# Attention, soft mixture of experts and MLP in one kernel: an eleventh load slot during attention, the last scores written where P will stand, two buffers for transposed P, and another order

## The chip, the cores and the metric

The program runs on one core of a Trainium2 chip. A core has a matrix engine (PE, with its weight loads shown as PEld), a vector engine (DVE), a scalar engine (ACT), a general engine (POOL) and a sequencer (SP) that here issues every DMA transfer. Each engine works through its own list of instructions in order and waits on semaphores. The metric is the device time of one execution in microseconds (us); lower is better.

## The reference, cut to what matters

```python
def _attn_ref(q, k, v):                 # q, k, v: 8 batches, 8 heads, 576 rows, 64 columns
    k_p = k.reshape(B, H, Sp, pool, D).mean(axis=3)      # 576 rows pooled to 72
    v_p = v.reshape(B, H, Sp, pool, D).mean(axis=3)
    scores = scale * np.matmul(q, k_p.transpose(0, 1, 3, 2))
    scores = scores - np.max(scores, axis=-1, keepdims=True)
    attn = np.exp(scores)
    attn = attn / (np.sum(attn, axis=-1, keepdims=True) + 1e-09)
    return np.matmul(attn, v_p)
def _moe_ref(x, phi, w1, w2):           # x: 4608 tokens of 512; 8 experts of 4 slots, F = 1024
    logits = x @ phi
    d = softmax of logits over the tokens; slot_input = d.T @ x
    for e in range(E):
        slot_out[e] = np.maximum(slot_input[e] @ w1[e], 0.0) @ w2[e]
    c = softmax of logits over the slots; return c @ slot_out
def _moe2_ref(x, w_in, w_out, s, b):    # 512 to 2048 to 512
    g = s * np.maximum(x @ w_in, 0.0) ** 2 + b
    return g @ w_out
```

## The kernel before, in words

Three stages follow each other on the same core: attention up to about 161 us, the experts (MoE) up to about 200 us, and the MLP to the end.

**Attention** goes over 36 tiles of 128 rows, t = 0 to 35, nine for each pair of batches (`pr, u = divmod(t, 9)`). A tile passes six steps, each a function. `st_A`: PE transposes q, ACT copies it to `qT`. `st_B`: PE multiplies with the pooled k (`kb`), DVE takes the maximum of each row (L413) and writes scores less maximum to `S` (L415). `st_C`: ACT takes the exponential in place (L423), DVE sums each row (L424) and inverts the sum (L426), POOL multiplies the two into P (L444). `S` has two buffers, for even and odd t, each with a 73rd column of 1e-9 behind the 72 scores, so that one sum over 73 columns gives the sum of the reference. P stands in six pair tiles `P2_0` to `P2_5` (two tiles of rows each) or in `Pm` (u = 0). `st_D`: PE transposes P, ACT copies it to `PT`. `st_E`: every second tile or so, PE multiplies two transposed tiles with `vpf` (pooled v already multiplied with phi), and ACT copies to `LT`. `st_F`: PE transposes that, DVE sums it into the logits `L`. `PT` has three buffers (`t % 3`), so that `st_D` of the next tile may stand ahead of the `st_E` that still reads the two before it.

After a batch's last F, `dispatch(b)` (a generator that is stepped by the letter r, or 6 and 7 for the last two batches) forms the slot inputs of that batch: PE L583, L588, L616 and L640 with DVE and ACT between. `prep(pr)` (stepped by p) pools k and v of the next pair: three additions for each chunk (L278, L282, L283), each chunk on POOL or DVE by a string such as PLAN1 (`kg0`: k chunk 0 on POOL; `kd1`: k chunk 1 on DVE; `K0`, `V0`: PE transposes of that chunk, L293).

The order of all this is written out by hand: FIRST and LOOP give the letters for each tile up to t = 27, TAIL for the rest. W3 in TAIL is three filler matmuls (L267) of the identity, which compute nothing.

**Loads.** All loads stand in one list, `loads`, and `pump()` issues its head as soon as a slot of 8 KB per partition is free; nothing passes the head. There are ten slots `ring` and three slots `raw` from the start. When the last reader of a pool of attention's tiles is written, TAIL closes the pool (Z: `pp1`, Y: `apb`, X1: `sc2`, X4: `apd`, X2: `apc`, X3: `apq`) and opens XR slots `x` over it, 3, 2, 1, 1 and 1 in the order Z, Y, X1, X4, X2; X3 opens a slot `brief`, and a second one follows behind attention. That makes 23 slots for the first 23 of the experts' 32 loads of 1 MB each. The other nine, and the first blocks of w_in and w_out, go into slots that the experts' matmuls set free.

**Experts.** The 32 weight blocks are taken in the order EORD: `w1` blocks with L1033, `w2` blocks with L1046 (into `sp_ps`) up to block NDIR - 1, and with L1049 (into `so_ps`, already folded) from NDIR on; L1021 adds what `sp_ps` held to `so_ps`. BEHIND says what else stands behind a block: t0 to t5 are PE transposes for the MLP (L968), c0 to c3 what these need, i and o conversions of w_in and w_out, and w2 two filler matmuls (L1015).

**MLP.** From L918 and L1136 on, PE goes through 96 steps of 18 matmuls (L1196) to the end.

## Time and profile before

| | |
|---|---|
| median of 3 runs | 643.15 us (642.7 to 644.52) |
| profiled execution, its own time | 644.16 us |
| span of that execution (first to last instruction) | 642.4 us |
| mean granted PE clock | 0.994 of full speed |
| busy: PE, DVE, ACT, POOL | 621.9, 450.1, 405.6, 303.4 us |
| bytes moved | 89.00 MB |

The profile shows one execution. A row of its timeline gives the start and the duration in us, the engine, the line of the kernel, the operation, the tiles that it writes and reads, how many such instructions are merged, and in brackets how long the engine had stood idle before and what ended that. Full PE clock is 2.4 GHz; 0.50 is 1.2 GHz. A matmul in f32 is shown as two rows, so eight rows are four matmuls.

### The profile page before, as it was taken

Reading aid. Unit: us, or ns where it says so; the run is one execution under the profiler, and the core shown is the slowest. Engines: PE = TensorE matmul, PEld = TensorE weight load, DVE = VectorE, ACT = ScalarE, POOL = GpSimd, SP = SyncE. Lnnn points to the kernel's source line nnn. Section 1 sums busy time; section 2 is a strip of 40 time slices with the busy share of each in tenths; the row PEclk is TensorE's granted clock in tenths of the full one; section 3 lists DMA queues with packets and bytes.
Section 4 is the critical chain, followed back from the end, with each engine's and each line's share of the span. In section 5 each row is a group of like instructions: output and inputs, shape, how many; then the busy total and the mean of one; then the engine's idle time right before and its main releaser. Section 6 shows DMA issues by size and latency. Waiting matters only on the chain.

```text
span 642.4 us, 13303 instructions
## 1 busy us (share of the span) xinstructions
PE 621.9 (97%) x5355; PEld 503.1 (78%) x5355; DVE 450.1 (70%) x722; ACT 405.6 (63%) x668; POOL 303.4 (47%) x241
## 2 busy tenths in 40 slices
PE   8879999998998999999999999999999999999997
PEld 7767778887545888888888888888888888888886
DVE  5768787897693787877658788967657554657444
ACT  3468788874374887756666656665656666565552
POOL 2987899534145344513153345351315332999100
PEclk9979999999999999999999999999999999999999
DMA  9999977679996202101111104021000000223323
GB/s 329 400 326 368 362 256 267 240 287 350 379 408 242 66 2 67 66 0 66 65 27 42 64 1 132 0 67 66 1 0 1 1 1 2 98 99 99 98 98 99
DMA packets 37389, 89.00 MB, mean 139 GB/s; under 512 B 6992, under 2 KB 15440, under 8 KB 37328
## 3 DMA queue, kind: packets, MB, share of 16 engines
q1 hardware_dynamic: 37328, 88.16, 38.4%
q8 instruction: 42, 0.69, 0.4%
q14 instruction: 19, 0.16, 0.1%
HBM read 78.71 MB, written 9.44 MB: 137 GB/s over the span
## 4 chain that ended last, share of the span: by engine, by line
PE 83%; DMA 6%; SPq 3%; DVE 3%; ACT 3%; issue 1%; POOL 1%; DVEq 0%; ACTq 0%; POOLq 0%
PE o L1196 61%; PE h L1136 5%; DMA x<-in_moe_w_dram 3%; PE l L1033 2%; PE sc L409 2%; SPq L152 2%; PE w L463 2%; DMA ring<-in_k_dram 2%; PE w L385 1%; PE w L616 1%; DMA qm<-in_q_dram 1%; PE w L489 1%; SPq L245 1%; POOL P L444 1%; PE w L514 1%
## 5 line engine op out<-in xcount | busy, mean ns | idle before, releaser
L1196 PE MATMUL o<-whi,gh 128*128 128x512 f32 x574 | 224.3, 391 | 0.6 <-DVE gh L1122 0.6
L1196 PE MATMUL o<-wlo,gh 128*128 128x512 f32 x574 | 224.0, 390 | 0.0
L1196 PE MATMUL o<-whi,gl 128*128 128x512 f32 x574 | 208.9, 391 | 0.0
L1164 DVE TENSOR_TENSOR gl<-r,gh 128x768 fp32r<-128x768 f32 (+1 forms) x97 | 105.8, 1092 | 112.1 <-ACT gh L1156 110.9
L1148 ACT ACTIVATE r<-h 128x768 f32<-128x768 f32 x94 | 76.7, 816 | 141.1 <-PE h L1136 139.2
L875 POOL TENSOR_TENSOR fr<-fr,xp 128x512 f32<-128x512 f32 x28 | 45.3, 1618 | 176.8 <-ACT fr L874 156.4
L1196 PEld LDWEIGHTS o<-whi,gl 128*128 128x128 f32 x574 | 107.7, 188 | 23.1 <-DVE gl L1164 0.4
L1196 PEld LDWEIGHTS o<-whi,gh 128*128 128x128 f32 x574 | 107.7, 188 | 20.9 <-issue 0.8
L1196 PEld LDWEIGHTS o<-wlo,gh 128*128 128x128 f32 x574 | 107.8, 188 | 18.9
L1212 DVE SCALAR_TENSOR_TENSOR part<-o,sb_t,part 128x512 f32<-128x512 f32 x143 | 96.4, 741 | 2.2 <-PE o L1196 2.1
L1149 ACT ACTIVATE r<-r 128x768 f32<-128x768 f32 x94 | 79.7, 848 | 3.0
L1156 ACT CAST gh<-r 128x768 fp32r<-128x768 f32 x94 | 78.5, 835 | 2.6
L1343 POOL TENSOR_TENSOR part<-part,wsum 128x512 f32<-128x512 f32 x36 | 53.2, 1521 | 15.1 <-ACT wsum L1337 15.1
L1136 PE MATMUL h<-cT,S 128*128 128x384 f32 x192 | 49.5, 338 | 0.0
L444 POOL TENSOR_TENSOR P<-S,sm 128x576 f32<-128x576 f32 x32 | 36.7, 1151 | 24.5 <-DVE sm L426 11.4
L1136 PEld LDWEIGHTS h<-cT,S 128*128 128x128 f32 x192 | 36.0, 188 | 8.3 <-DVE S L1232 0.2
L415 DVE TENSOR_TENSOR S<-sc,mx 128x576 f32<-128x576 f32 x36 | 27.3, 758 | 11.0 <-POOL P L444 6.6
L413 DVE TENSOR_REDUCE mx<-sc 128x8 f32<-128x576 f32 x36 | 26.4, 734 | 6.9 <-PE sc L409 6.4
L424 DVE TENSOR_REDUCE sm<-S 128x8 f32<-128x584 f32 x36 | 27.1, 752 | 5.7 <-ACT S L423 5.4
L387 ACT COPY qT<-w 128x512 f32<-128x512 f32 x36 | 21.0, 586 | 13.7 <-PE sc L409 10.1
L409 PE MATMUL sc<-kb,qT 64*64 64x72 f32 x1152 | 27.4, 234 | 0.3 <-ACT kb L310 0.2
L423 ACT ACTIVATE S<-S 128x576 f32<-128x576 f32 x36 | 24.7, 687 | 4.4 <-DVE S L415 4.1
(263 smaller groups left out, 863.6 us busy)
## 6 DMA issues: line engine op xcount, KB each, us to landing
ring<-in_moe_w_dram SPq DMA_DIRECT2D x13, 1024.0 KB, 6.7
x<-in_moe_w_dram SPq DMA_DIRECT2D x10, 1024.0 KB, 7.4
out_dram<-part SPq DMA_DIRECT2D x31, 256.0 KB, 2.9
ring<-in_q_dram SPq DMA_DIRECT2D x7, 1024.0 KB, 15.3
raw<-in_moe_w_in_dram SPq DMA_DIRECT2D x7, 1024.0 KB, 5.4
raw<-in_moe_w_out_dram SPq DMA_DIRECT2D x7, 1024.0 KB, 5.0
ring<-in_k_dram SPq DMA_DIRECT2D x9, 768.0 KB, 9.0
raw<-in_moe_w_dram SPq DMA_DIRECT2D x6, 1024.0 KB, 7.8
```

What stands on the lines that cost most here:

```text
L409: nc.tensor.matmul(out=sc[r, x, KP * i:KP * i + KP], lhsT=qT[p, i, r], rhs=kb[p, n, :], start=True, stop=True)
L415: nc.vector.tensor_tensor(out=S[:, :, :, 0:KP], in0=scv, in1=mx.unsqueeze(3).to_broadcast([128, 2, 4, KP]), op=ALU.subtract)
L444: nc.gpsimd.tensor_tensor(out=o, in0=S, in1=rb, op=ALU.mult)
L875: nc.gpsimd.tensor_tensor(out=fr, in0=fr, in1=xp, op=ALU.mult)
L1136: nc.tensor.matmul(out=h[x][:, 0:384] if i == 0 else h[:, x, 0:384], lhsT=Sw[:, f, :], rhs=cT(c, 384), start=True, stop=True)
L1148: nc.scalar.activation(out=r, in_=h[:, :, 0:384], func=ACTF.Relu)
L1149: nc.scalar.activation(out=r, in_=r, func=ACTF.Square)
L1156: nc.scalar.copy(out=gh_t[i], in_=r)
L1164: nc.vector.tensor_tensor(out=gl[:, x], in0=r[:, x], in1=gh[:, x].bitcast(F32), op=ALU.subtract)
L1196: nc.tensor.matmul(out=o_t[tt], lhsT=l[:, x, 128 * c:128 * c + 128], rhs=r, start=(fi == 0 and n == 0), stop=(fi == GROUPS[g] - 1 or (tt = ...
L1212: nc.vector.scalar_tensor_tensor(out=p, in0=o_t[tt], scalar=sb_t[:, 0:1], in1=p, op0=ALU.mult, op1=ALU.add)
L1343: nc.gpsimd.tensor_tensor(out=p, in0=p, in1=wsum, op=ALU.add)
```

## The change

Eight kilobytes per partition are set aside as a slot `x0` before attention, an eleventh one beside the ten of `ring`; once no load of q, k or v is waiting, it serves the experts' weights. XR's last entry goes from 1 to 0, so the number of slots for the experts' loads stays 23.

From t = 30 on (TZ) `st_B` writes scores less maximum to the place of P2 where P of that tile will stand (`P_of`), ACT works there in place, and POOL multiplies in place. That place has no 73rd column, so the sum takes two instructions: L446 sums 72 columns into `se`, whose second column holds 1e-9, and L447 sums the two. The two `S` buffers go from the pool `sc2` to `pp1`, which Z closes. `PT` has two buffers, so each `st_E` has to stand ahead of the next `st_D`.

The strings that set the order are all written anew. PLAN1 has k chunk 0 instead of k chunk 1 on DVE. TAIL has 21 filler matmuls instead of 15, BEHIND seven instead of ten. EA goes from 3 to 2 (two `w2` blocks instead of three ahead of the last six `w1` blocks), NDIR from 31 to 30 (two blocks with L1049 instead of one), KEEP keeps other slots for scratch, WOPOS goes from 27 to 28.

```diff
-PLAN1 = "kg0 kd1 kg0|kg2 kg2||K0 vg0 kd1|vg0 vg2 K1|K2 vg2 vd1 V0 vd1|V2 V1"
+PLAN1 = "kd0 kg1 kd0|kg2 kg2||vg0 kg1|vg0 vg2 K1 K0 vd1|K2 vg2 V0 vd1|V2 V1"
...
-KEEP = (1, 3, 3, 6)
-XR = (3, 2, 1, 1, 1)
+KEEP = (1, 2, 3, 6)
+TZ = 30
+XR = (3, 2, 1, 1, 0)
...
-    free_slots, free_extra, free_raw = deque(ring), deque(), deque(raw)
+    xctx = ExitStack()
+    x0 = xctx.enter_context(tc.tile_pool(name="x0", bufs=1)).tile([128, 2048], F32, name="x0")
+    free_slots, free_extra, free_raw = deque(ring + [x0]), deque(), deque(raw)
...
         pool, slot, _ = where.pop(key)
+        if slot is x0 and not any(z[0][0] in ("q", "k", "v") for z in loads):
+            pool = free_extra
...
-        S_t[t] = S = S_buf[t % 2]
-        nc.vector.tensor_tensor(out=S[:, :, :, 0:KP], in0=scv, in1=mx.unsqueeze(3).to_broadcast([128, 2, 4, KP]), op=ALU.subtract)
+        S = P_of(t) if t >= TZ else S_buf[t % 2][:, :, :, 0:KP]
+        S_t[t] = S
+        nc.vector.tensor_tensor(out=S, in0=scv, in1=mx.unsqueeze(3).to_broadcast([128, 2, 4, KP]), op=ALU.subtract)
...
+        if t >= TZ:
+            nc.vector.tensor_reduce(out=se[:, :, :, 0], in_=S, axis=AX.X, op=ALU.add)
+            nc.vector.tensor_reduce(out=sm, in_=se, axis=AX.X, op=ALU.add)
+        else:
+            nc.vector.tensor_reduce(out=sm, in_=S_buf[t % 2], axis=AX.X, op=ALU.add)
         nc.vector.reciprocal(out=sm, in_=sm)
...
+        nc.gpsimd.tensor_tensor(out=S if t >= TZ else P_of(t), in0=S, in1=rb, op=ALU.mult)
...
-    PT = apc.tile([128, 4, 3, 128], F32, name="PT")
+    PT = apc.tile([128, 4, 2, 128], F32, name="PT")
```

**First place: PE where pair 1 begins (t = 8 to 10).** `kp` is pooled k, `qm` the part of q that the first tile of a pair (t = 9) needs, `P_1` the pair tile of t = 3 and 4. Lines of the change count from its own file: L300, L392, L416, L471, L496, L521 are L293, L385, L409, L463, L489, L514 of before. Before:

```order
L293 MATMUL w<-ident,kp 64x128 x3
L385 MATMUL w<-ident,ring_79 128x128 x4
L463 MATMUL w<-ident,P_1_107 128x128 x4
L489 MATMUL w<-PT,vpf_154 32x256 x4
L495 MATMUL w<-PT_159,vpf_154 32x64 x4
L293 MATMUL w<-ident,kp 64x128 x3
L385 MATMUL w<-ident,qm 128x128 x4
L463 MATMUL w<-ident,P_1_107 128x128 x4
L471 MATMUL w<-ident,P_1_107 64x128 x2
L409 MATMUL sc<-kb_127,qT 64x72 x16
L514 MATMUL w<-ident,LT 128x128 x2
L409 MATMUL sc<-kb_127,qT 64x72 x16
```

The change, from the same tile on:

```order
L392 MATMUL w<-ident,ring_79 128x128 x4
L496 MATMUL w<-PT,vpf_161 32x256 x4
L502 MATMUL w<-PT_166,vpf_161 32x64 x4
L471 MATMUL w<-ident,P_1_111 128x128 x4
L521 MATMUL w<-ident,LT 128x128 x2
L300 MATMUL w<-ident,kp 64x128 x6
L471 MATMUL w<-ident,P_1_111 128x128 x4
L478 MATMUL w<-ident,P_1_111 64x128 x2
L416 MATMUL sc<-kb_131,qT 64x72 x16
L392 MATMUL w<-ident,qm 128x128 x4
L416 MATMUL sc<-kb_131,qT 64x72 x16
```

The transposes of the first k chunk went from the front behind the step F (L521) and stand with those of the second; the transposes of `qm` went behind a step D (L471, L478) and a step B (L416); and the step E (L496) stands ahead of the next step D.

**Second place: the experts' loads on SP, and PE at the end of the experts.** SP before, from the loads that Z opens on:

```order
L152 DMA x<-in_moe_w_dram 128x2x1024 x3
L152 DMA ring_82<-in_moe_w_dram 128x2x1024
L152 DMA x<-in_moe_w_dram 128x2x1024 x5
L152 DMA brief_2952<-in_moe_w_dram 128x2x1024
L152 DMA brief_2964<-in_moe_w_dram 128x2x1024
L152 DMA ring_78<-in_moe_w_dram 128x2x1024
```

SP in the change:

```order
L155 DMA x<-in_moe_w_dram 128x2x1024 x3
L155 DMA raw_64<-in_moe_w_dram 128x2x1024
L155 DMA x<-in_moe_w_dram 128x2x1024 x4
L155 DMA brief_2974<-in_moe_w_dram 128x2x1024
L155 DMA brief_2986<-in_moe_w_dram 128x2x1024
L155 DMA ring_80<-in_moe_w_dram 128x2x1024
```

Ahead of the two `brief` loads stand four loads into slots of closed pools instead of five; the fifth went ahead of Z, into `x0`. PE before, up to the last `w2` block:

```order
L968 MATMUL ct<-ident,ring_75 128x128 x3
L1015 MATMUL xt<-ident 128x128 x2
L1046 MATMUL sp_ps<-raw_65,ring_77 32x512 x4
L1015 MATMUL xt<-ident 128x128 x4
L1046 MATMUL sp_ps<-x,ring_77 32x512 x2
L1046 MATMUL sp_ps<-x,z_all 32x512 x2
L1046 MATMUL sp_ps<-x,ring_77 32x512 x4
L1049 MATMUL so_ps<-x,ring_77 32x128 x8
L1049 MATMUL so_ps<-x,z_all 32x128 x8
L1021 MATMUL so_ps<-sp,sel_62 32x128 x4
```

PE in the change (L973, L1020, L1051, L1054, L1026 are L968, L1015, L1046, L1049, L1021):

```order
L973 MATMUL ct<-ident,ring_82 128x128 x3
L1020 MATMUL xt<-ident 128x128 x2
L1051 MATMUL sp_ps<-raw_65,ring_76 32x512 x4
L1051 MATMUL sp_ps<-ring_75,ring_76 32x512 x2
L1051 MATMUL sp_ps<-ring_75,z_all 32x512 x2
L1054 MATMUL so_ps<-x,ring_76 32x128 x16
L1026 MATMUL so_ps<-sp,sel_62 32x128 x4
L1054 MATMUL so_ps<-x,ring_76 32x128 x8
L1054 MATMUL so_ps<-x,z_all 32x128 x8
```

Four filler matmuls between the last blocks are gone, the last two blocks instead of the last one go to `so_ps`, and L1026 stands ahead of the last block.

**Third place: DVE at the last two tiles' sums (t = 34 and 35).** Before:

```order
L424 TENSOR_REDUCE sm<-S_130 128x8
L426 RECIPROCAL sm<-sm 128x8
L648 COPY si_all<-w 128x128
L516 TENSOR_REDUCE L<-w 128x2x32
L576 TENSOR_REDUCE md<-L 128x32
L424 TENSOR_REDUCE sm<-S_131 128x8
L426 RECIPROCAL sm<-sm 128x8
L585 TENSOR_REDUCE md<-w 32x1
```

The change (L450, L655, L523, L583, L592 are L426, L648, L516, L576, L585):

```order
L446 TENSOR_REDUCE se<-P_3_113 128x8
L447 TENSOR_REDUCE sm<-se 128x8
L450 RECIPROCAL sm<-sm 128x8
L655 COPY si_all<-w 128x128
L523 TENSOR_REDUCE L<-w 128x2x32
L583 TENSOR_REDUCE md<-L 128x32
L446 TENSOR_REDUCE se<-P_3_113 128x8
L447 TENSOR_REDUCE sm<-se 128x8
L450 RECIPROCAL sm<-sm 128x8
L592 TENSOR_REDUCE md<-w 32x1
```

Each tile from t = 30 on has one more instruction on DVE, L447; nothing else moved at this place.

## Rows read from the trace of the kernel before

**Rows 1.** Stretches: length; busy us of PE, PEld, DVE, ACT, POOL; clock; DMA; GB/s.

```profile
40.40:47.20 6.80, 5.20 (x76) 4.25 (x76) 1.95 (x5) 2.32 (x7) 6.45 (x6) 0.50 0.94 340
...
54.00:118.00 64.00, 61.13 (x1314) 49.36 (x1314) 50.13 (x106) 51.91 (x128) 57.82 (x53) 1.00 0.88 309
...
134.00:145.00 11.00, 10.91 (x258) 9.04 (x258) 10.19 (x21) 7.54 (x20) 4.51 (x4) 1.00 0.65 249
...
161.00:181.00 20.00, 19.75 (x296) 11.08 (x299) 14.78 (x37) 8.77 (x21) 3.40 (x4) 1.00 1.01 385
```

**Rows 2.** Chain that ended last, in order of time, 181 to 200 us.

```profile
181.01 17.43 DMA x<-in_moe_w_dram
...
199.13 0.22 PE so_ps L1021 x8
```

**Rows 3.** Timeline of PE, the end of the experts.

```profile
188.78 1.16 PE L1015 MATMUL xt<-ident 128*128 128x128 f32 x8
189.87 1.48 PE L1046 MATMUL sp_ps<-raw,ring 128*32 128x512 f32 x10
...
195.91 1.06 PE L1046 MATMUL sp_ps<-x,ring 128*32 128x512 f32 x8
197.19 0.64 PE L1049 MATMUL so_ps<-x,ring 128*32 128x128 f32 x16 [0.21 <-DMA x<-in_moe_w_dram]
198.48 0.65 PE L1049 MATMUL so_ps<-x,z_all 128*32 128x128 f32 x16 [0.65 <-DMA x<-in_moe_w_dram]
```

**Rows 4.** Timeline of SP, 144 to 154 us: issues of loads.

```profile
144.23 9.57 SPq L152 DMA_DIRECT2D x<-in_moe_w_dram  x5
```

**Rows 5.** Timeline of PE, 36 to 48 us.

```profile
39.69 0.49 PE L293 MATMUL w<-ident,kp 128*64 128x128 f32 x3 [1.56 <-DVE kp L283]
42.00 1.09 PE L385 MATMUL w<-ident,qm 128*128 128x128 f32 x4 [1.81 <-DMA qm<-in_q_dram]
...
44.30 1.24 PE L409 MATMUL sc<-kb,qT 64*64 64x72 f32 x32
...
47.25 0.52 PE L293 MATMUL w<-ident,kp 128*64 128x128 f32 x3
```

**Rows 6.** The page's DMA issues: line, count, KB each, median us to landing.

```profile
ring<-in_k_dram SPq DMA_DIRECT2D x9, 768.0 KB, 9.0
```

**Rows 7.** Timeline of POOL, 36 to 57 us.

```profile
36.92 1.82 POOL L278 TENSOR_TENSOR ring<-ring 128x768 f32<-128x768 f32 x1
40.60 2.26 POOL L444 TENSOR_TENSOR P<-S,sm 128x576 f32<-128x576 f32 x2 [1.86 <-DVE sm L426]
42.81 0.99 POOL L282 TENSOR_TENSOR ring<-ring 128x384 f32<-128x384 f32 x1
43.89 0.59 POOL L283 TENSOR_TENSOR vp<-ring 128x192 f32<-128x192 f32 x1
...
53.16 1.15 POOL L444 TENSOR_TENSOR P<-S,sm 128x576 f32<-128x576 f32 x1 [2.85 <-ACT PT L476]
```

**Rows 8.** Timeline of DVE, 36 to 52 us.

```profile
45.60 0.76 DVE L413 TENSOR_REDUCE mx<-sc 128x8 f32<-128x576 f32 x1 [4.28 <-PE sc L409]
...
49.42 1.71 DVE L278 TENSOR_TENSOR ring<-ring 128x768 f32<-128x768 f32 x1
```

**Rows 9.** Who PE waited for, 54 to 145 us: us in total, times, longest.

```profile
PE w L463 <- POOL ring L278: 0.9, 1, 0.9
```

**Rows 10.** DVE by line, 118 to 150 us: busy us, mean ns, idle before.

```profile
L426 DVE RECIPROCAL sm<-sm 128x8 f32<-128x8 f32 x10 | 2.0, 203 | 0.3
```

**Rows 11.** Chain that ended last, in order of time, 145 to 162 us.

```profile
146.18 0.44 DVE md L576
...
147.63 0.87 PE w L267 x6
```

**Rows 12.** Timeline of PE, 157 to 162 us.

```profile
159.52 0.66 PE L640 MATMUL w<-si_all,vps 72*64 72x32 f32 x16 [0.55 <-ACT si_all L635]
```

**Rows 13.** Timeline of DVE, 159 to 162 us.

```profile
160.50 0.29 DVE L651 TENSOR_TENSOR si_all<-w,m_all 128x128 f32<-128x128 f32 x1
```

More of the change, by code (lines that the diff above doesn't have):

```diff
@@ L17 @@
 PSUM = bass.MemoryType.PSUM
[L19 to L24 removed]
+OPS = 'o0 a0 a1 o1 o0 c0 o1 u0 c1 h0 w1 u1 g0'
+WIPOS, WOPOS = 25, 28
+BEHIND = {9: 'c0', 13: 'i0 c3', 27: 't5 w2', 22: 't3 t4 w3', 17: 't1 t2', 12: 'c1 c2', 16: 'o0', 20: 'w1', 10: 't0', 15: 'i1', 8: 'w1', 23: 'o1'}
+TAIL = "r p B26 r E22 C25 r A28 D23 r F22 r B27 C26 A29 D24 p r r E24 B28 C27 p A30 r D25 D26 B29 A31 F24 r r C28 B30 E26 D27 p r C29 p p F26 A32 B31 r E27 C30 Z r W1 A33 D28 r F27 C31 A34 W1 p B32 D29 r r B33 r r p E29 C32 A35 D30 F29 C33 r B34 B35 D31 r W1 C34 E31 r D32 F31 6 C35 W3 D33 Y W2 6 W1 E33 m m 6 6 F33 D34 6 m D35 X1 6 X4 E35 W1 6 F35 7 6 W3 m 7 W2 7 7 m 7 6 M2 7 W2 7 M3 X2 M5 7 M4 W1 W3 7 X3"
 BUSY = 2
[L26 removed]
+NDIR, EA = 30, 2
 CUT = 1
 LOOP = (
[3 rows of a table removed]
[3 rows of a table added]
     "r r E B C D A r F p r",
[2 rows of a table removed]
[2 rows of a table added]
     "F B p r A E C r D",
[2 rows of a table removed]
[2 rows of a table added]
 )
 FIRST = {
[8 rows of a table removed]
[8 rows of a table added]
 }
 PREP = (4, 10, 19)
[L51 removed]
+PLAN1 = "kd0 kg1 kd0|kg2 kg2||vg0 kg1|vg0 vg2 K1 K0 vd1|K2 vg2 V0 vd1|V2 V1"
 PLAN2 = "kg2|kg2 kg0|kg0 kg1 K2|kg1||vg2 vg2 K0|vg0|V2 vg0|vg1 vg1 V0 K1|V1"
@@ L199 @@
     BRIEF, NBRIEF = 8, 2
-    NSLOT = NRING + NRAW + sum(XR) + NBRIEF
+    NSLOT = NRING + 1 + NRAW + sum(XR) + NBRIEF
     for w, e, hf in EORD[:BRIEF] + EORD[BRIEF + NBRIEF:NSLOT] + EORD[BRIEF:BRIEF + NBRIEF] + EORD[NSLOT:]:
@@ L252 @@
     nc.gpsimd.memset(L_all, -3.0e38)
-    S_buf = [sc2.tile([128, 2, 4, KP + 1], F32, name=f"S{i}", bufs=1) for i in range(2)]
+    S_buf = [pp1.tile([128, 2, 4, KP + 1], F32, name=f"S{i}", bufs=1) for i in range(2)]
+    se = ap2.tile([128, 2, 4, 2], F32, name="se", bufs=1)
+    nc.vector.memset(se, 1e-9)
     for S in S_buf:
@@ new lines, in st_B, with P_of @@
+        S = P_of(t) if t >= TZ else S_buf[t % 2][:, :, :, 0:KP]
+        S_t[t] = S
+        nc.vector.tensor_tensor(out=S, in0=scv, in1=mx.unsqueeze(3).to_broadcast([128, 2, 4, KP]), op=ALU.subtract)
+    def P_of(t):
+        pr, u = divmod(t, 9)
+        if u == 0:
+            P = P_t[t] = (ap1 if pr % 2 else apb).tile([128, H, KP], F32, tag="Pm", name="Pm")
+            return P.rearrange("p (i x) k -> p x i k", x=2)
+        j = (u - 1) % 4
+        n = 4 * pr + (u - 1) // 2
+        if n not in P2_t:
+            P2 = P2_all[n % 6 if pr < NPR - 1 else n % 4]
+            P2_t[n] = P2
+            t0 = t - j % 2
+            P_t[t0], P_t[t0 + 1] = P2[:, 0], P2[:, 1]
+            pair_t[t0 + 1] = [P2[:, 0], P2[:, 1]]
+        return P2_t[n][:, :, 4 * (j % 2):4 * (j % 2) + 4, :]
@@ new lines, in st_C @@
+    def st_C(t):
+        S = S_t.pop(t)
+        nc.scalar.activation(out=S, in_=S, func=ACTF.Exp)
+        sm = ap2.tile([128, 2, 4], F32, tag="sm", name="sm")
+        if t >= TZ:
[3 more added lines that the diff above has]
+            nc.vector.tensor_reduce(out=sm, in_=S_buf[t % 2], axis=AX.X, op=ALU.add)
+        nc.vector.reciprocal(out=sm, in_=sm)
+        rb = sm.unsqueeze(3).to_broadcast([128, 2, 4, KP])
+        nc.gpsimd.tensor_tensor(out=S if t >= TZ else P_of(t), in0=S, in1=rb, op=ALU.mult)
@@ L463, in st_D @@
             nc.tensor.transpose(out=pa[:, 128 * c:128 * c + 128], in_=Pf[:, 128 * c:128 * c + 128], identity=ident)
-        assert not held or held[0][0] > t - 3
+        assert not held
         if last:
-            assert not held
             held.append((t - x, t))
@@ L473, in st_D @@
                 )
-        nc.scalar.copy(out=PT[:, :, t % 3], in_=pa.rearrange("p (c x) -> p c x", c=4))
+        nc.scalar.copy(out=PT[:, :, t % 2], in_=pa.rearrange("p (c x) -> p c x", c=4))
         if last:
@@ L710 @@
     running, preps = [], []
-    xctx = ExitStack()
     def extra(n, last=False):
```

32 lines of the change are left out of this document (1 added, 31 removed), and 30 rows, old and new, of tables (FIRST, LOOP).

## The prediction

> **What bounds the kernel now.** I read the page's slices first, then the chain that ended last, then stretches between the places that the chain names, and in each stretch the timeline of the engine that waits. The MLP runs from 204 us on with PE never idle, in steps that the change does not touch, so whatever moves the start of the MLP moves the end by as much. Three things ahead of it matter.
>
> At the end of the experts the chain is a transfer: it lies on the last block of `w2` from 181.01 us for 17.43 us [rows 2]. PE waits for the two halves of that block, 0.21 and 0.65 us [rows 3]. But PE is close behind: from 161 to 181 us it is busy 19.75 of 20 us, while the DMA engines are full too (share 1.01, 385 GB/s) [rows 1]. So two limits lie within about a microsecond of each other, and PE has filler matmuls in this stage: four of them from 188.78 to 189.87 us, 0.27 each [rows 3].
>
> Attention is a matter of several engines. From 54 to 118 us PE is busy 61.13 of 64 us and POOL 57.82 [rows 1]; PE's longest wait up to 145 us is 0.9 us, for POOL [rows 9]. From 134 to 145 us DVE is busy 10.19 of 11 us and PE 10.91 [rows 1]. The one loose place is at pair 1: PE waits 1.56 us for pooled k and 1.81 us for `qm` [rows 5], and behind these waits the granted clock stands at 0.50, which is 1.2 GHz, from 40.4 to 47.2 us [rows 1]. DVE idles 4.28 us there [rows 8] and POOL 1.86 us [rows 7].
>
> **The change part by part.** Times are differences to before, minus is earlier.
>
> *The eleventh slot.* Five loads go out from 144.23 us on as attention's pools close [rows 4]; in the change it is four, and the fifth goes into `x0`, long before, where the DMA engines have room (share 0.65 from 134 to 145 us [rows 1]). From there on the transfers stand back to back, so one load fewer is worth 1.05 MB at 385 GB/s, 2.7 us, to every load behind it, the last one too. That is more than PE can use. With no wait left, PE's work decides: the two waits go, -0.86 [rows 3]; BEHIND has three fillers fewer, 3 x 0.27 = -0.82 [rows 3]; the second block with L1049 takes two groups of 0.64 us instead of one L1046 group of 1.06 us, +0.2 [rows 3]. That PE now adds `sp_ps` ahead of the last block gives nothing if PE is the limit, since the work is the same. Sum **-1.5**. Bounds: if the last load still lands where it did, measured from the start of the experts, only the 0.22 us of that addition (L1021, from 199.13 us, behind the last L1049 [rows 2]) could be won, so -0.2; if fillers and waits hid more than they cost, PE follows the loads and gets -2.7.
>
> *Pair 1.* Three moves act together. First, `qm` comes later: with an eleventh slot for q, k and v one more chunk of k is issued ahead of it, 768 KB [rows 6]; at the 385 GB/s above that is 2.0 us in a full queue, so it lands at about 43.8 instead of just before 42.00 us [rows 5]. Second, PE has more to do ahead of it: step D (two groups) and one step B went in front, so `qm` is wanted later by what these take. Third, k chunk 1 is pooled on POOL instead of DVE: the last two additions fall behind POOL's addition that ends at 38.74 us, into its idle 1.86 us, and take 0.99 + 0.59 us there [rows 7]; pooled k is ready at about 40.4 instead of 39.6 us. Walking PE through the new order: it stands still from 38.1 us (39.69 less its wait of 1.56 [rows 5]) to 40.4. From 42.00 us, at half clock, the four transposes of `qm` and the six of a D took 2.30 us, 0.23 each, and two B with two transposes of F 2.95 us up to 47.25 [rows 5], so a B 1.24; at full clock that is 0.115 and 0.62. Six transposes of k, six of D and a B are then 2.0 us; PE waits for `qm`, 0.1 us behind its landing, and from 43.9 us does its four transposes and the second B, 1.1 us. At 45.0 us it is at the place that it reached at 47.25 before, -2.3. If the clock falls as before and stays down all the way, PE is at `qm` at 44.4 us and at that place at 46.6, -0.7. The clock should fall again, since PE's idle stretch ahead of 40.4 us grows; but behind it PE has hardly a wait, where before it waited 1.81 us in the middle. In addition DVE's addition of a v chunk (1.71 us from 49.42 us [rows 8]) now stands in its idle 4.28 us, so the next two products of POOL, at 53.16 us before [rows 7], come about 3 us earlier, and POOL doesn't hold PE back behind this place. Between these I take **-1.7**, nearer to the full clock because of the missing wait. Ends: -2.3 and, if all that is won is lost again to POOL by 118 us, 0; for a dearer wait on `qm` +0.5. From 54 to 134 us the work of each engine is the same and only its order differs; I take 0 for it, with half of PE's waits there, 0.8 us, either way.
>
> *The scores in place.* From t = 30 on each tile has one more instruction on DVE, L447 with 8 results from 16 numbers. No row shows it; the nearest is the reciprocal of the same 8 numbers, 203 ns [rows 10], and the gap of 0.04 us to the instruction that waits for it. Five of the six lie in the stretch in which DVE has hardly a gap, so the last tile's reciprocal comes 5 x 0.24 = 1.2 us later, and `md` of batch 6, with four of them ahead, 1.0 us. What reaches the end of attention is less. The chain goes from `md` (146.18 us) to PE, whose next work holds three fillers of 0.87 us [rows 11]; TAIL puts two of these three ahead of that wait, so 1.0 - 0.6 = 0.4 remains for what follows, and 0.8 for batch 6's own matmuls, whose `md` passes DVE once more behind all five. I take **+0.6**; ends 0 (PE has slack) and 1.2. The wait of `st_B` for POOL's product from an `S` buffer disappears for these tiles, but PE is the later engine there: nothing.
>
> The Vector Engine (DVE) Microarchitecture Reference of the Trainium skill gives in its section on measured stream behaviour about 75 ns for each instruction plus 1.04 ns for each column. By that page L447 would be an estimated 0.09 us and this term about half. The reciprocal's 203 ns on 8 columns disagrees with it, and I go by the row.
>
> *Fillers at the end of attention.* One filler more, and three that stood behind it, now stand ahead of the last L640. PE is free at 158.97 us and waits 0.55 us for `si_all` until 159.52 us [rows 12]. Four fillers of 0.29 us (three take 0.87 [rows 11]) end at 160.1 us, so L640 ends 0.6 us later, and DVE's L651, which stood at 160.50 us [rows 13] right behind L640's 160.18 us, moves to about 160.8: **+0.3**. Ends 0 and 0.6.
>
> *The rest.* `PT` with two buffers costs nothing by itself where PE reaches E only when ACT has copied; the order was rewritten so that D always follows E. OPS changes only the order in which ACT and POOL instructions are written, not their order on an engine. The block order (EA) and WOPOS move which blocks wait; with 2.7 us in hand at the loads I take nothing.
>
> **Sum:** -1.5 - 1.7 + 0.6 + 0.3 = -2.3 us. The profiled execution took 644.16 us with a span of 642.4, and the median is 643.15; the profiled one would go to 641.9 and its span to 640.1. Against the median I forecast 640.9 us. A measurement of this kernel tells apart about 0.3%, 1.9 us, so this is just outside of it, below 641.2.
>
> **The rivals.** *Pair 1 gives little, or POOL takes it back.* For it: POOL is busy 57.82 of 64 us behind it [rows 1], and one of PE's waits there is for a POOL addition [rows 9]. Against it: POOL is ahead by as much. Then -1.5 - 0.2 + 0.9 = -0.8: 642.4 us, no change that can be told.
>
> *The last load still ends the experts.* The first block of w_in stands third in the list behind attention and wants a `ring` slot, while `x0` and others are free for weights; nothing passes it, and the transfers could idle. Against it: the loads stand well ahead of PE by then. Then -0.2 - 1.7 + 0.9 = -1.0: 642.2 us.
>
> *The order is better throughout*, PE's waits from 54 to 134 us go and the clock returns early: -2.3 - 0.8 - 0.6, 639.5 us.
>
> *The other sign: two `PT` buffers.* Each E must stand ahead of the next D, so it comes sooner behind the copies by ACT (two for each of 20 E). If PE waits w us at each, 20 w is added; it ends slower than before by 0.3% from w = (2.3 + 1.9) / 20 = 0.21 us on; at 0.25 us it is +2.7, 645.9 us. For it: in the first place that the order shows, a D that lay between went behind its E. Against it: PE's longest waits before name no `PT` [rows 9], and on average as many matmuls stand between the two as before.
>
> **How the numbers follow.** Forecast 0.50 (its own range 639.9 to 642.0), better throughout 0.14, pair 1 gives little 0.20, last load 0.08, `PT` 0.08. Faster by over 0.3%: four fifths of the forecast and the better case, 0.54. Slower: 0.08. Within: 0.38. The range reaches from the sum of the better case with the loads' bound (-4.6: 638.6) to that of the weak cases with the larger tail (-0.8 + 0.9: 643.3) and leaves out the `PT` case and what is beyond.
>
> **What the profile after would show.** Right: no wait of PE for `x` at the end of the experts and the last load landing some microseconds ahead of its L1054; PE at `qm` at about 43.9 us; the first L1038 (L1033 of before) 0.8 us earlier than before (the last three terms) and the MLP's first L923 (L918 of before) 2.3 us earlier. Wrong: PE waiting for `PT` in its list of waits, a longer stretch at clock 0.50, the DVE stretch of the last six tiles late by over 1.2 us, or DMA shares under 1 behind 161 us.

## The result: slower, 647.27 us

The change took 647.27 us (median of 6 runs, 645.42 to 649.5) against 642.94 for the kernel before: ratio 1.0064, 95% interval 1.0052 to 1.0077. The forecast was 640.9 us. The profiled execution took 648.4 us with a span of 646.5, 4.1 us longer than that of before.

How far the work is at some places shows where the time went. The first five rows are the start of a tile's row maximum on DVE (L413, L420 in the change), the last two a start on PE; all are starts in the timelines:

| place | before, us | change, us | difference |
|---|---|---|---|
| t = 9 | 54.60 | 52.49 | -2.1 |
| t = 18 | 87.20 | 88.74 | +1.5 |
| t = 26 | 114.83 | 116.74 | +1.9 |
| t = 29 | 124.49 | 126.05 | +1.6 |
| t = 35 | 143.13 | 147.18 | +4.1 |
| first L1038 | 161.29 | 165.76 | +4.5 |
| first L923 | 200.63 | 204.72 | +4.1 |

By this pair of profiles pair 1 gave what was forecast, but a second profile of the change (below) is only 0.7 us early at t = 9. Of the 6.2 us between t = 9 and t = 35 only the 0.6 for the second sum were forecast, and the experts gave 0.4 us instead of 1.5.

Timeline of PE in the change where pair 1 begins, which answers to [rows 5]:

```profile
42.22 0.84 PE L300 MATMUL w<-ident,kp 128*64 128x128 f32 x6 [1.11 <-POOL kp L290]
...
44.92 0.63 PE L392 MATMUL w<-ident,qm 128*128 128x128 f32 x4 [0.54 <-DMA qm<-in_q_dram]
...
46.14 0.52 PE L300 MATMUL w<-ident,kp 128*64 128x128 f32 x3
```

Pooled k came at 42.2 us, 1.8 later than the forecast's walk had it, and `qm` at 44.9, 1.0 later. Still PE waits 0.54 us for `qm` here instead of 1.81, and is at the next k transposes at 46.14 us instead of 47.25. The granted clock stays at 1.00 from 34.3 to 71.9 us. In the second profile of the change the same wait is longer, and the next k transposes begin at 47.20 us:

```profile
45.47 0.63 PE L392 MATMUL w<-ident,qm 128*128 128x128 f32 x4 [2.25 <-DMA qm<-in_q_dram]
```

Stretches of the change, which answer to [rows 1], with two more (length; busy us of PE, PEld, DVE, ACT, POOL; clock; DMA share; GB/s):

```profile
54.00:118.00 64.00, 59.78 (x1228) 48.55 (x1227) 47.04 (x99) 49.64 (x121) 56.23 (x51) 0.97 0.88 305
71.90:75.20 3.30, 3.30 (x32) 2.82 (x35) 2.29 (x5) 2.02 (x4) 2.53 (x2) 0.50 1.07 354
134.00:145.00 11.00, 11.00 (x293) 9.46 (x281) 9.41 (x24) 7.83 (x20) 3.75 (x4) 1.00 0.87 323
...
161.00:181.00 20.00, 19.16 (x311) 12.10 (x315) 14.10 (x44) 6.84 (x19) 3.90 (x7) 1.00 0.89 317
...
162.00:164.60 2.60, 2.60 (x44) 2.25 (x32) 1.89 (x7) 0.82 (x3) 1.32 (x3) 1.00 0.47 93
```

No engine became the bound: from 54 to 118 us every one is less busy than before. The granted clock stood at 0.50 (1.2 GHz) for 3.4 us from 71.9 us on, which is worth 1.7 us; and behind 161 us, where the DMA engines were full before, their share is 0.89. PE's waits from 54 to 145 us, which answer to [rows 9] (us in total, times, longest):

```profile
PE w L471 <- POOL ring L289: 1.6, 1, 1.6
PE sc L416 <- DVE L L523: 1.5, 1, 1.5
PE w L471 <- issue: 0.9, 1, 0.9
PE sc L416 <- issue: 0.8, 1, 0.8
```

Read by name these are waits for POOL, for DVE and for nothing ("issue"). Their rows in PE's timeline tell more:

```profile
67.86 0.38 PE L471 MATMUL w<-ident,P 128*128 128x128 f32 x2
69.85 0.44 PE L471 MATMUL w<-ident,P 128*128 128x128 f32 x2 [1.61 <-POOL ring L289]
...
89.34 0.65 PE L416 MATMUL sc<-kb,qT 64*64 64x72 f32 x25
90.76 0.35 PE L416 MATMUL sc<-kb,qT 64*64 64x72 f32 x7 [0.77 <-issue]
...
126.41 0.38 PE L521 MATMUL w<-ident,LT 128*128 128x128 f32 x2
128.31 0.73 PE L416 MATMUL sc<-kb,qT 64*64 64x72 f32 x32 [1.52 <-DVE L L523]
```

PE stands still in the middle of a step: two rows (one matmul) of D's four transposes of one tile P are done, then 1.61 us nothing, then the others; and in the middle of a step B. The rest of a group that reads the same tiles has no data to wait for. The wait of [rows 9] looks the same in the timeline of before:

```profile
68.71 0.38 PE L463 MATMUL w<-ident,P 128*128 128x128 f32 x2
70.02 0.44 PE L463 MATMUL w<-ident,P 128*128 128x128 f32 x2 [0.93 <-POOL ring L278]
```

The experiments go after this.

DVE by line, 118 to 155 us (busy us, mean ns, idle before):

```profile
L450 DVE RECIPROCAL sm<-sm 128x8 f32<-128x8 f32 x11 | 2.2, 203 | 0.4
...
L447 DVE TENSOR_REDUCE sm<-se 128x8 f32<-128x16 f32 x6 | 1.0, 171 | 0.6
```

SP's issues of loads (start, duration), which answer to [rows 4], one of before and then those of the change, and the timeline of PE in the change at the end of the experts, as [rows 3]:

```profile
157.75 3.42 SPq L152 DMA_DIRECT2D brief<-in_moe_w_dram  x2
```

```profile
134.45 2.63 SPq L155 DMA_DIRECT2D x<-in_moe_w_dram  x3
...
148.19 7.89 SPq L155 DMA_DIRECT2D x<-in_moe_w_dram  x4
162.36 3.27 SPq L155 DMA_DIRECT2D brief<-in_moe_w_dram  x2
...
173.32 0.37 SPq L155 DMA_DIRECT2D ring<-in_moe_w_in_dram  x1
```

```profile
200.23 1.08 PE L1054 MATMUL so_ps<-x,ring 128*32 128x128 f32 x32 [1.50 <-DMA x<-in_moe_w_dram]
...
202.79 0.64 PE L1054 MATMUL so_ps<-x,z_all 128*32 128x128 f32 x16 [0.63 <-DMA x<-in_moe_w_dram]
```

Four loads go out instead of five, but SP is then done at 156.08 us and waits 6.3 us until X3 opens the `brief` slot at 162.36 (before, 3.95 us up to 157.75); the transfers run dry meanwhile (93 GB/s from 162.0 to 164.6 us, above). The first `brief` load is issued 3.4 us ahead of the first experts' matmul in the change and 3.5 us ahead of it before, so with attention's end it moves as PE does. PE still waits for the last load.

### The profile page after: what moved, and what is told of

The parts are those of the page before. It is cut to its first block, busy times and chain, and to the rows that moved or that the text cites. A ratio compares the mean times of both kernels' runs of the same rounds, so it can differ in the third digit from the quotient of the medians.

```text
span 646.5 us, 13383 instructions
## 1 busy us (share of the span) xinstructions
PE 623.2 (96%) x5385; PEld 505.8 (78%) x5385; DVE 450.7 (70%) x729; ACT 405.9 (63%) x668; POOL 303.5 (47%) x241
## 4 chain that ended last, share of the span: by engine, by line
PE 83%; DMA 5%; DVE 4%; ACT 3%; POOL 1%; issue 1%; SPq 1%; DVEq 0%; ACTq 0%; POOLq 0%
PE o L1201 61%; PE h L1141 5%; DMA x<-in_moe_w_dram 3%; PE sc L416 2%; PE l L1038 2%; PE w L392 2%; PE w L471 1%; DMA ring<-in_k_dram 1%; PE w L274 1%; DMA qm<-in_q_dram 1%; PE w L623 1%; PE w L496 1%; PE w L300 1%; POOL P L452 1%; ACT PT L481 1%
## 5 line engine op out<-in xcount | busy, mean ns | idle before, releaser
L452 POOL TENSOR_TENSOR P<-S,sm 128x576 f32<-128x576 f32 x26 | 30.4, 1174 | 17.4 <-DVE sm L450 11.2
L449 DVE TENSOR_REDUCE sm<-S 128x8 f32<-128x584 f32 x30 | 22.7, 756 | 10.5 <-ACT S L443 10.3
L420 DVE TENSOR_REDUCE mx<-sc 128x8 f32<-128x576 f32 x36 | 26.5, 736 | 4.7 <-PE sc L416 4.4
L416 PE MATMUL sc<-kb,qT 64*64 64x72 f32 x1152 | 27.0, 231 | 2.6 <-DVE L L523 1.5
L416 PEld LDWEIGHTS sc<-kb,qT 64*64 64x64 f32 x1152 | 21.5, 134 | 8.6 <-issue 4.2
L423 DVE TENSOR_TENSOR S<-sc,mx 128x576 f32<-128x576 f32 x30 | 22.7, 758 | 7.4 <-POOL P L452 4.0
```

Source lines behind the costliest of these rows:

```text
L416: nc.tensor.matmul(out=sc[r, x, KP * i:KP * i + KP], lhsT=qT[p, i, r], rhs=kb[p, n, :], start=True, stop=True)
L420: nc.vector.tensor_reduce(out=mx, in_=scv, axis=AX.X, op=ALU.max)
L452: nc.gpsimd.tensor_tensor(out=S if t >= TZ else P_of(t), in0=S, in1=rb, op=ALU.mult)
```

## The experiments

Before was timed anew beside each group (medians 643.30 to 643.89 us), so ratios are compared. 0.001 is 0.64 us.

### The data alone, and what of it costs

The change with all order strings of before; in FIRST's row for t = 8 one E stands ahead of D, the only place where the order of before broke the rule that two `PT` buffers need.

```diff
-PLAN1 = "kd0 kg1 kd0|kg2 kg2||vg0 kg1|vg0 vg2 K1 K0 vd1|K2 vg2 V0 vd1|V2 V1"
+PLAN1 = "kg0 kd1 kg0|kg2 kg2||K0 vg0 kd1|vg0 vg2 K1|K2 vg2 vd1 V0 vd1|V2 V1"
-    8: "p B C A E D F",
+    8: "B p C A E D F r",
...
-NDIR, EA = 30, 2
+NDIR, EA = 31, 3
```

> The change with every order string of before (FIRST, LOOP, PLAN1, TAIL, BEHIND, EA, NDIR, KEEP, WOPOS, OPS; in FIRST's row for t = 8 one E stands ahead of D, which two PT buffers need): slot x0, scores in place and two PT buffers alone. Theory 'the order': the 4.1 us by which the MLP starts later in the change come from the rewritten strings, since PE's step B was 2.1 us early at t = 9 and 1.9 us late at t = 26, before any in-place tile; then this runs like before or better by up to the 1.5 us of the eleventh slot, 641.5 to 643.3 us. Rival 'the data': the six L447 and pool pp1 (Z), which now waits for the product of tile 29 because the S buffers lie in it, cost the 2 to 2.5 us that are lost between t = 26 and t = 35, and the loads behind Z come later; then 644.5 to 645.5 us.

646.52 us, 1.0047 (1.0034 to 1.0060). The data cost most of the loss by themselves, and at one place: PE is 0.8 us late at t = 6 and 3.4 us at t = 7, and 3.5 at t = 30. Its timeline there:

```profile
45.42 1.08 PE L392 MATMUL w<-ident,qm 128*128 128x128 f32 x4 [4.42 <-DMA qm<-in_q_dram]
```

So "the data" was nearer on the total, which it had 1.0 us too low, and wrong on the mechanism: from t = 30 to the first experts' matmul only 0.8 us more are lost. It is `qm`: one more slot lets the two small loads of s and b and one more chunk of k go ahead of it, and its first half is issued at 37.45 us instead of 31.30.

Next, slot `x0` for the experts' weights only:

```diff
-    free_slots, free_extra, free_raw = deque(ring + [x0]), deque(), deque(raw)
+    free_slots, free_extra, free_raw = deque(ring), deque([x0]), deque(raw)
```

> Slot, scores in place and two PT buffers with the strings of before, as in the run of the data alone, but slot x0 serves only the experts' weights, so that no load of k goes ahead of qm. Theory 'qm': in the run of the data alone PE waited 4.42 us for qm at 45.42 us and was 3.5 us late from there on, which was all of its loss; the rest was +0.8 us up to the first experts' matmul and -1.57 us in the experts. Then PE at t = 9 stands as before and the time is 643.3 + 0.8 - 1.6 = 642.5 us, 641.9 to 643.0. Rival 'two PT buffers or the S pool cost in the middle': PE is late by t = 20 again, 644 us or more.

644.54 us, 1.0010 (1.0001 to 1.0019): 2.4 us of the loss were `x0` in the early loads. PE's wait for `qm` is nearly that of before again (2.25 us against 1.81). The 642.5 us expected are not reached, in part since the gain in the experts was counted against one execution of before (below). The time is the one that the rival named, but at t = 20 PE is 0.8 us late against the first profile of before and 0.15 against the second, so a loss in the middle isn't shown.

```profile
42.59 1.09 PE L392 MATMUL w<-ident,qm 128*128 128x128 f32 x4 [2.25 <-DMA qm<-in_q_dram]
```

Then without L447, that is, without the 1e-9 in these tiles' sums:

```diff
-            nc.vector.tensor_reduce(out=se[:, :, :, 0], in_=S, axis=AX.X, op=ALU.add)
-            nc.vector.tensor_reduce(out=sm, in_=se, axis=AX.X, op=ALU.add)
+            nc.vector.tensor_reduce(out=sm, in_=S, axis=AX.X, op=ALU.add)
```

> As the run with x0 for weights only, and for the tiles from t = 30 on the sum takes one instruction: L447, which adds 1e-9 to the sum, is left out. Theory 'L447 costs some tenths': the six instructions of about 0.2 us stand on the way of the last tiles, where the step B of t = 35 came 0.4 us and the first experts' matmul 0.8 us later; 0.4 to 0.8 us go, 641.7 to 642.1 us. Rival 'PE or POOL is as late': no difference to the run with x0 for weights only, within 0.3 us.

643.65 us, 0.9999 (0.9989 to 1.0010). Six L447 cost 0.9 us by the medians. Slot, scores in place and two `PT` buffers without them together cost nothing and bring nothing.

### One part undone in the change

TAIL of before (its string as in the kernel before):

> The change with TAIL of before. Theory 'the order, late part': the 2.5 us lost between t = 26 and the first experts' matmul (+1.9 to +4.5 us) come from TAIL's rewriting (PE waits 1.52 us for L523 at 128.31 us and has six fillers more); they go, 644.5 to 645 us. Rival 'the data': DVE with L447 and Z behind tile 29's product cost them whatever TAIL says, 646.8 to 647.5 us.

645.54 us, 1.0028 (1.0015 to 1.0040): better by 2.3 us. From t = 29 on it loses 0.8 us to the first experts' matmul instead of 2.9. The profiles tell where: from t = 29 to t = 35 the change loses 2.5 us in both of its profiles, with pauses (see below) of 1.5 and 1.9 us in that stretch; seven other versions with TAIL of the change, in which no pause of 0.4 us or more falls there, lose 0.8 to 0.9, and this run, with TAIL of before, 0.4.

BEHIND, EA, NDIR, KEEP, WOPOS and OPS of before:

> The change with BEHIND, EA, NDIR, KEEP, WOPOS and OPS of before. The experts took 38.96 us from their first matmul to the MLP's first L923, against 39.34 before, and the last load still ended them. Theory 'the last load ends the experts': block order and fillers weigh nothing beside it but the 0.2 us of L1026, which stands ahead of the last block in the change; 647.2 to 647.6 us. Rival 'the w_in block in the list': in the change w_in's first block was issued at 173.32 us, 5.5 us behind the load ahead of it, and the transfers stood still for 1.3 us; if the new block order causes it, 645.9 to 646.5 us.

646.57 us, 1.0050 (1.0036 to 1.0064): the intervals overlap, so no difference can be told. The block of w_in was issued at 173.50 us here, as late as in the change, so the rival that blamed the new block order fell.

FIRST, LOOP and PLAN1 of before:

> The change with FIRST, LOOP and PLAN1 of before (one E ahead of D at t = 8): eleventh slot for all loads, TAIL and the experts' strings of the change. Theory 'each place by itself': PE is 3.5 us late from qm on, as in the run of the data alone, 1.6 us more than the change is at t = 26, so 648.5 to 649 us. Rival 'TAIL of the change is what loses in the tail only behind its own early order': 646.5 to 647.3 us.

645.97 us, 1.0038 (1.0025 to 1.0050), where 648.5 to 649 had been expected (an earlier expectation for the same strings, on the theory that t = 26 would stand where it stood before, was 645.3 to 646.3; it stands 2.0 us later): PE waits 5.18 us for `qm` and is 2.9 us late at t = 9, but only 2.4 at t = 28. Of the 5.0 us by which the new early strings are ahead of these at t = 9 (-2.1 against +2.9), 0.5 are left at t = 28 (+1.8 against +2.4).

`x0` for weights only, as above, in the change:

> The change as it is, but slot x0 serves only the experts' weights. The early strings alone made the kernel before 1.4 us faster, and within the change they cost 1.7 us; with x0 for weights only, the data alone cost 0.9 us instead of 3.0. Theory 'late qm': the new early order gains where qm comes in time, so the parts add: 643.5 - 1.4 (early) + 0.9 (data) + 2.3 (TAIL) + 0.5 (experts) = 645.8 us, 645.3 to 646.3. Rival 'the new early order has room for the late qm, as the forecast's walk had it': no difference to the change, 646.8 to 647.6 us.

645.86 us, 1.0026 (1.0013 to 1.0039): as forecast, 2.4 us better, the same as in the data alone. But the runs lie from 643.25 to 646.79 us. In its profile `qm` is there in time, and PE is 2.8 us early at t = 9, where the change was 2.1 and 0.7 us early.

### One part alone, and the best parts together

The kernel before with FIRST, LOOP and PLAN1 of the change:

> The kernel before with FIRST, LOOP and PLAN1 of the change, and nothing else: ten slots, qm lands where it did (41.9 us). Theory 'the middle loses by itself': PE is up to 3 us early at t = 9, and the new order gives it back between t = 9 and t = 26 (4.0 us in the change, with a wait of 1.6 us for a POOL addition at 70 us and a stretch at half clock behind it), so 643.5 to 645 us. Rival 'the late qm sets the loss off': without it the gain at t = 9 stays, 640.5 to 641.5 us.

642.19 us, 0.9979 (0.9970 to 0.9988): faster than both kernels, the one version here that is. PE is 1.5 us early at t = 9 and 0.8 from t = 29 to the experts. "The late `qm` sets the loss off" was nearer.

The kernel before with TAIL of the change:

> The kernel before with TAIL of the change and nothing else: S with 73 columns and the S buffers in the pool that X1 closes, three PT buffers. Theory 'TAIL costs by itself': it has six fillers more and another order, and took 2.3 us within the change (run with TAIL of before); 645.3 to 646.2 us. Rival 'TAIL is dear only with the second sum and the later Z': within 0.6 us of before.

644.29 us, 1.0016 (1.0004 to 1.0027): between the two expectations, 0.9 us by itself.

Early and experts' strings of the change, `x0` for weights, one sum, TAIL of before:

> The parts that paid or cost nothing: early strings and experts' strings of the change, slot x0 for weights only, scores in place with one sum (L447 and its 1e-9 left out), two PT buffers, TAIL of before. Theory 'the parts add': 643.5 - 1.4 (early strings) + 0 (data without L447) - 0.5 (the experts took 37.27 us with these strings in one run and 37.8 with those of before) = 641.6 us, 641.2 to 642.2. Rival 'the experts' strings of the change cost, as the run with those of before has it (0.7 us faster)': 642.2 to 642.9 us.

643.55 us, 1.0008 (0.9990 to 1.0026). The parts don't add: 12 runs lie from 641.17 to 646.65 us, some near 642.7, some near 646. Something makes executions of one and the same kernel differ by 3 us and more.

### What differs between executions

The kernel before, profiled again:

> The kernel before once more, for a second profile of it. In its first profile PE waited 0.98 us for the last loads of the experts, behind a step of 4.1 us between two landings that follow each other by 2.55 us elsewhere, and the experts took 39.34 us. Theory 'that step belonged to that execution': the experts take 37.8 us here, as in the run of the early strings alone, whose experts are the same, and PE waits for no load at their end. Rival 'ten slots make PE wait': about 1 us of waits again, 39 us or more.

The experts took 38.37 us. PE's waits from 161 to 204 us, of this execution and then of the early strings alone, whose experts are those of before, too:

```profile
PE o L1196 <- DVE gh L1122: 0.6, 1, 0.6
PE o L918 <- DVE sot L1093: 0.4, 1, 0.4
PE so_ps L1049 <- DMA x<-in_moe_w_dram: 0.4, 1, 0.4
```

```profile
PE o L1196 <- DVE gh L1122: 0.6, 1, 0.6
PE o L918 <- DVE sot L1093: 0.4, 1, 0.4
```

0.4 us and none, where [rows 3] have 0.86; the experts took 37.83 us with the early strings alone. So at least half of the wait that the forecast counted on belonged to one execution. Against these two profiles of the same experts the change's 38.96 us are no gain but a loss of 0.6 and 1.1 us.

The change, profiled again:

> The change once more, for a second profile. Theory 'single executions': the wait of 1.52 us ahead of a step B at 128.31 us, and 1.50 of the 2.13 us for the last loads of the experts, belong to the first execution and are not here; the stretch at half clock behind 70 us may or may not be. Rival 'they are the kernel's': both waits again within 0.3 us, at the same instructions.

Its own time was 648.72 us. PE's waits from 54 to 145 us and from 161 to 206 us:

```profile
PE w L471 <- POOL ring L289: 1.9, 1, 1.9
PE w L392 <- issue: 0.7, 1, 0.7
PE w L623 <- issue: 0.7, 1, 0.7
PE w L471 <- issue: 0.6, 1, 0.6
...
PE so_ps L1054 <- DMA x<-in_moe_w_dram: 1.6, 2, 1.0
```

The wait near 70 us and, with 0.5 us less, those for the loads came again; that at 128 us is down to 0.42 us, others are new; and the clock stays at 1.00 near 72 us, though this execution took 648.72 us. Neither expectation was right as a whole.

Five filler matmuls ahead of D of tile 10, where PE waits near 70 us:

```diff
     9: "F C p D B r A E",
+    15: "F B p r A E C r w5 D",
```

> The change with five filler matmuls (1.4 us at full clock) ahead of step D of tile 10, where PE waits 1.61 us for POOL at 69.85 us. Theory 'the wait drops the clock': the idle stretch is filled, the clock stays at 1.00 behind it, the upper group of times (648.4 to 649.5) goes and the median is 645.4 to 646.2, with a scatter under 2 us. Rival 'the clock falls for other reasons, or the scatter comes from elsewhere': both groups stay, 646.5 to 648 us.

647.03 us, 1.0046 (1.0026 to 1.0065), 644.19 to 649.22: no help. PE's timeline says why, for the idle stretch wasn't filled:

```profile
67.97 0.39 PE L275 MATMUL w<-ident 128*128 128x128 f32 x2
69.63 1.05 PE L275 MATMUL w<-ident 128*128 128x128 f32 x8 [1.27 <-issue]
70.52 0.60 PE L472 MATMUL w<-ident,P 128*128 128x128 f32 x4
```

L275 is the fillers, which read nothing but the identity. One of the five runs, then PE stands still, and then the rest runs and D without a wait. In the change it was one matmul of D, then the pause: the pause stands behind the same number of instructions, whatever they are. So it is not POOL. That half clock behind this pause makes the scatter is refuted by the change's second profile, 648.72 us with the clock at 1.00 there.

What fits is PE's supply of instructions. The page counts 42 packets on the queue q8 of kind "instruction", 0.69 MB, 16 KB each; PE has 5385 matmuls, as many weight loads and 127 rows of its sequencer, on average 259 rows for each packet. Counted over all these rows in order of time, the four pauses of the change stand behind row 1729, 1986, 2754 and 4290. The steps between these are 257, 768 and 1536, that is one, three and six times 256 to within one row: each pause stands behind the 193rd or 194th place of a block of 256. A fifth, of 1.69 us at 30.83 us, ahead of pair 1 and with half clock for 3.4 us behind it, stands behind the 193rd, too, and so does that of before at 70.02 us behind the 194th. The wait of 0.47 us for POOL's product at 54.50 us stands behind the 146th; it is a wait for data. The queue's row in the stretches 67.0 to 68.6 and 125.9 to 127.0 us (packets, MB, share of 16 engines):

```profile
q8 instruction: 1, 0.02, 4.2%
```

```profile
q8 instruction: 1, 0.02, 5.8%
```

One packet each, of 1.07 and 1.02 us (share by 16 by the length), started at 67.32 and 125.94 us by the packets' records; PE goes on 2.5 and 2.4 us behind that. The test of it is every block of all 20 profiles: PE passes no such place less than 2.2 us behind the start of the block's packet, and the pauses of 0.4 us or more there stand where that distance is 2.2 to 2.9 us. Where a packet started earlier there is none (waits for a copy by ACT or a load that happen to fall at the 195th place or so aside).

The early strings alone with the same fillers:

> The kernel before with FIRST, LOOP and PLAN1 of the change and the same five fillers ahead of step D of tile 10. Theory 'the wait drops the clock': the early strings alone were mostly in the lower group already (641.5 to 642.4 in 9 of 11 runs); the two runs at 643.1 and 644.0 go, median 641.8 to 642.2. Rival 'fillers cost, since they end behind POOL': 642.5 to 643 us.

643.67 us, 1.0000 (0.9990 to 1.0010): twenty instructions took the whole gain of those strings. They don't fill the pause here either: it falls behind the first of the five, so the fillers' own 1.4 us are enough to explain the 1.5.

The same and the experts' strings of the change:

> As the early strings with filled wait, and BEHIND, EA, NDIR, KEEP, WOPOS and OPS of the change; ten slots. Theory 'loads and PE lie level at the end of the experts': with three fillers fewer PE would be up to 0.8 us earlier, and with ten slots the loads, 2.55 us each, hold it back; no gain, 641.8 to 642.4. Rival 'fillers are what PE spends there': 0.5 to 0.8 us faster, 641.1 to 641.5.

644.18 us, 1.0011 (0.9998 to 1.0023): no gain, as expected, but 1.8 us above the expected range, which had taken the fillers to cost nothing; its profile has pauses of 1.82, 1.25 and 1.07 us.

64 instructions more at the start of PE's list:

```diff
     warm(14)
+    ps = bank()
+    for _ in range(16):
+        nc.tensor.matmul(out=ps[:, 0:8], lhsT=ident, rhs=ident[:, 0:8], start=True, stop=True)
     first_k()
```

> The change with 16 matmuls of 8 columns more at the very start (64 instructions on PE, about 1 us, where PE waits for k anyway). Theory 'instruction blocks': PE gets its instructions in blocks of 256, and where a block comes late PE stands still at the same count in the block; so the waits of 0.85 us near 62.8 and of 1.6 to 1.9 us near 69.8 us leave step D of tiles 8 and 10 and appear 64 instructions (16 matmuls) earlier in the program, or not at all, and the median moves by 0.5 to 2 us either way though the work is the same. Rival 'POOL': the wait stays ahead of step D of tile 10, 1.3 to 1.9 us, and the time is that of the change, 646.8 to 647.6 us.

646.90 us, 1.0051 (1.0034 to 1.0068). The 16 matmuls cost far more than meant: t = 0 stands 4.8 us later than in the change. At t = 35 it is 0.8 us later. The pause has left D of tile 10, though the time lies in the range of the rival; PE's waits from 54 to 145 us, and its timeline:

```profile
PE sc L416 <- issue: 1.4, 2, 0.8
PE w L647 <- ACT si_all L642: 0.5, 2, 0.3
PE w L392 <- issue: 0.4, 1, 0.4
```

```profile
76.77 0.72 PE L416 MATMUL sc<-kb,qT 64*64 64x72 f32 x31
78.30 0.27 PE L416 MATMUL sc<-kb,qT 64*64 64x72 f32 x1 [0.81 <-issue]
```

The pauses now cut steps B, again behind the 193rd or 194th place, and with one of 0.4 us ahead of L392 sum to 1.8 us instead of 4.8 (1.61 + 1.52 + 0.85 + 0.77). POOL as their cause is excluded. As all of it also ran later against the loads, the drop in their sum isn't shown to come from the shift.

With 32 such matmuls, and with 16 in the early strings alone:

> The same with 32 such matmuls (128 instructions, about 2 us; PE may be 0.5 us late at its first transposes of k). Theory 'instruction blocks': the waits stand 128 instructions earlier in the program than in the change or vanish, and the median moves by 0.5 to 2 us either way. Rival 'POOL': the wait stays ahead of step D of tile 10, and the time is 646.8 to 648 us.

> The early strings alone (the kernel before with FIRST, LOOP and PLAN1 of the change) with 64 instructions more at the start. Five fillers (20 instructions) ahead of step D of tile 10 made that kernel 1.4 us slower though they stood in a wait. Theory 'instruction blocks': the waits of 1.97 us at 31.6 and 1.32 us at 69.5 us move 64 instructions earlier, and the time moves by 0.5 to 2 us either way, to 640.5 to 644 us. Rival 'no effect of the count of instructions': 641.9 to 642.5 us, waits at the same instructions.

652.97 us, 1.0151 (1.0130 to 1.0172), 11.6 us later at t = 0 than the change; and 646.07 us, 1.0030 (1.0012 to 1.0048), 4.3 us later at t = 0 than the early strings alone. The late start hides what was to be seen in the times. In both no wait of over 0.5 us stands ahead of D of tile 10 any more.

## Why the prediction was wrong

By the first profiles the forecast of -2.3 us is 6.4 us away from the +4.1 measured: 5.6 of these lie between t = 9 and t = 35, 1.1 in the experts, 0.1 at the end of attention, and -0.4 at pair 1.

**The eleventh slot, -1.5.** The step that failed is "from there on the transfers stand back to back, so one load fewer is worth ... 2.7 us, to every load behind it". The loads behind it begin with `brief`, which X3 opens at the end of attention; the load that went ahead of Z only makes SP wait longer for that, 6.3 us in the change. The 13 loads from `brief` on (two and nine of the experts, w_in and w_out) are the same as before, and the last lands 40.4 and 40.3 us behind the first issue of `brief` in the two profiles of the change, 40.7 and 39.7 in those of before. And at least half of the 0.86 us of waits was of one execution. PE's own work did shrink, by more than the 0.6 us forecast (fillers and blocks): 37.79 us for the experts with `x0` for weights and the strings of before, with no wait for a load, and 36.73 us with the strings of the change in the run with 64 instructions more, where PE waits 0.4 us for a load, 1.1 us less. In the change the loads take that back: 38.96 us, 2.1 of them waits for loads. That is the rival "the last load still ends the experts". Besides, the S buffers now lie in the pool that Z closes, and Z's three loads wait for POOL's product of tile 29 (134.45 instead of 128.65 us); the section on the change names the move, and the forecast gave it no cost.

**Pair 1, -1.7.** The sum came out in one profile, -1.1 us at the next k transposes and -2.1 at t = 9, and not in the other, 0 and -0.7, so the agreement is in part luck. `qm`'s place behind a chunk of k was seen, and 1.0 us too early in the first profile and 1.5 in the second; that two small loads would pass as well, so that `qm` is issued at 36.72 us instead of 31.30, was not. Half clock did not follow in the first profile, and came at 46.02 us, for 3.4 us, in the second. Not seen either is what the late `qm` cost: with `x0` kept from it the change is 2.4 us faster, of which the profiles show 0.7 and 2.1 us at t = 9.

**54 to 134 us, 0.** "The work of each engine is the same and only its order differs; I take 0 for it" is the step that cost the sign: it left no room for waits that depend on neither work nor data. The chain of waits was read by the names of the releasers, and [rows 9] put PE's 0.9 us down to POOL; that wait is such a pause, too, split within D like that of the change. Between t = 9 and t = 35 the change lost 6.2 us. The pauses from 54 to 145 us are 4.8 us against 1.5 (0.93 and 0.54, of which 0.54 at 77.05 us is "issue"), 3.3 more; half clock from 71.9 us, 1.7; L447, 0.9 at the most, for between the two profiles that differ by it alone only 0.2 of that fall between t = 29 and t = 35. That leaves 0.3 to 1.0 us, and TAIL's new order has its 0.5 in it (0.9 against 0.4 without pauses, above). This is the account of one pair of executions. Between the second profiles of both kernels 4.8 us are lost from t = 9 to t = 35; the pauses up to there (one at 145.34 us among them) are 5.0 against 2.1 us, so 3.0 more, and half clock didn't fall there, so 1.8 us are left for L447, TAIL's order and what stays open.

**L447, +0.6.** Right within its ends: 0.9 by the medians, from 171 ns for one. By the Vector Engine (DVE) Microarchitecture Reference of the Trainium skill, section on measured stream behaviour, one would take an estimated 0.09 us; the trace has almost twice that.

**Fillers and TAIL, +0.3.** Too small: TAIL, new order and fillers together, costs 0.9 us alone and 2.3 in the change. At the end of attention itself (t = 35 to the first L1038) 0.4 us were lost, by all of its parts.

**Two `PT` buffers.** Nothing, by the run without L447: the order of before broke their rule in one place, so the rival that counted 20 steps E had no ground. This could have been counted before the run.

**The range.** Its lower end is a wrong sum: the better case, -3.7, with the loads' bound, 1.2 more, is -4.9, not -4.6. That changes nothing here, for the time came out above the other end, 643.3.

**Open.** That the pauses come with PE's instruction packets is shown by their places and by the distance to the packets' starts; why a packet starts late, and why the pauses are longer with the new early strings, is not. Waits of 0.4 us or more at such places from 54 to 145 us sum to 0.4 to 2.2 us in the profiles with the early strings of before and to 1.3 to 4.9 in those with the new ones (the runs with instructions added at the start left out). The half clock behind the pause near 70 us came in three of ten profiles with the new ones. That pauses make what TAIL costs beyond its own 0.9 us is read from single profiles, and no run shows it.
